# First feed-forward of an attention and two-layer expert chain: operand halves and Strassen sums of the weights kept in DRAM, products chained in PSUM, scores negated

## Chip, cores and metric

The kernel runs on one core of a Trainium2 chip. The metric is the device time of one execution in microseconds (us), as the median of several runs. A change of 0.3% (8.6 us) is about the least that a measurement of this kernel tells from none.

## What is computed

```python
# attention over blocks of 32 queries with 8 memory keys: q, k, v of 4 x 8 heads x 768 x 64
scores = scale * np.matmul(q_c, k_full.transpose(0, 1, 3, 2))
scores = scores - np.max(scores, axis=-1, keepdims=True)
a = np.exp(scores)
a = a / (np.sum(a, axis=-1, keepdims=True) + 1e-09)
out[:, :, c_start:c_end] = np.matmul(a, v_full)
...
# first feed-forward, x is 3072 x 512, w_gate and w_val 512 x 1536, w_out 1536 x 512
gate = 1.0 / (1.0 + np.exp(-(x @ w_gate)))
val = x @ w_val
return (gate * val @ w_out).astype(np.float32)
...
# second: 8 experts of 512 x 1024 x 512, gates P normalised 8 times by rows and columns
h = np.maximum(x @ w1[e], 0.0)
ye = h @ w2[e]
out += P[:, e:e + 1] * ye
```

The weights of the first feed-forward come as float64 (its mean values are made as float64 in the inputs), and the kernel turns them into float32 with integer operations on the chip.

## The kernel before

Every float32 matrix product is made of three matmuls on rounded halves (`mm3`, L74): an operand x is kept as a rounded part h and a rest l = x - h, and `wh*xh + wh*xl + wl*xh` is summed in PSUM. `operand` (L106) makes the two halves: ACT casts h, and another engine (POOL for weights, mostly) subtracts it. "Split" means this below.

The 3072 tokens are 8 chunks of 384 (c = 0 to 7). Attention of a chunk is 4 head pairs (`attention`, L178): score matmuls, DVE scales and masks (L205), takes the row maxima (L208) and negates them (L209), ACT takes the exponential with that bias (L212), DVE the reciprocal of the sums, POOL scales (L216), then transposes and the product with v. It is a generator of four or five pieces, which `hook()` calls at times that `schedule` lists, so that it fills in beside the feed-forward.

**Stage A** (about 0 to 320 us in the trace) has attention of chunks 0 to 3 and the first feed-forward of chunks 0 and 1. `convert(f)` (L250) turns one of 12 groups f of 128 hidden units from float64 to float32: for each of three weights (i = 0 gate, 1 value, 2 out) ACT takes the magnitude, DVE does five operations (L264 to L271), POOL adds (L273), and SP stores the result in the DRAM scratch `wd`. 24 steps follow one another, chunk 0 with f = 0 to 5, chunk 1 with f = 0 to 5, chunk 0 with f = 6 to 11, chunk 1 with f = 6 to 11. `plain_first` (L336) splits the three weights of its step from the float32 tiles in SBUF (for i = 2 and f of 6 or more it loads them from `wd`), does 24 matmuls (`ps`), a sigmoid in three ACT operations (`sg`), and makes `g`, `gh`, `gl`; `plain_second` (L366) does 12 matmuls with the out weight (`px`) one step later. The conversions 2 to 11 stand behind given steps, by the tables

```python
AN = (0, -1, -1, -1, 0, 2, 0, 0, 0, 0)
CV = (0, 1, 2, 3, 6, 8, 9, 11, 12, 14)
```

The k-th conversion is written behind step `CV[k]`, and where `AN[k]` is not negative its DVE work may be issued only after the `gl` of step `CV[k] - AN[k]`.

**Stage B** (about 320 to 862 us) has the first feed-forward of chunks 2 to 7, in three blocks b = 1, 2, 3 of two chunks, and attention of chunks 4 to 7 beside the first two blocks. Each block takes six pairs p of groups f. For a pair, three loads `wl` from `wd` bring the float32 weights; `w1_operands` (L125) makes seven Strassen operands each for gate and value (on POOL four sums of quarters, `combine`, and four splits), and two splits make the out weights. `strassen` (L452) multiplies seven products, each into a PSUM bank of its own (`p_g`, `p_v`), and DVE adds them up (L462, `ca` to `ce`). `second` (L494) does the 48 matmuls with the out weight.

**Behind it** (862 us to the end) come the normalisation of P and the experts. There the second feed-forward already keeps its split operands and Strassen sums in DRAM scratch (`w1k`, `w2k`), reloads them, and chains products in PSUM, with ACT copies (`ca`, `cb`, `ce`, L709 to L720).

Transfers of weights and of q, k, v are all issued by SP, in the order in which the program is laid out. The tile framework orders each engine's instructions, and a buffer's next use waits for its last reader.

Of the kernel before, what the change touches and what calls it, by code (L numbers as in the profile page):

```python
# [10 lines left out]
F32 = mybir.dt.float32  # L11
F32R = mybir.dt.float32r
# [9 lines left out]
QB = 96  # L22
# [38 lines left out]
def moe_chain(ctx: ExitStack, tc: tile.TileContext, qkv, mask, wa, wg, wb, out):  # L61
# [28 lines left out]
    def slot(tag, name, n=512, dt=F32):  # L90
        return big.tile([128, 512], dt, tag=tag, name=name, bufs=SLOTS[tag])[:, 0:n]
# [11 lines left out]
    def tmp(name, n=512):  # L103
        return tp.tile([128, 512], F32, tag="c", name=name)[:, 0:n]
# [39 lines left out]
    def w1_load(nm, pool, kept):  # L144
# [3 lines left out]
        return w1_sets(t)  # L148

    with ExitStack() as c1:  # L150
        wc = c1.enter_context(tc.tile_pool(name="wc", bufs=7))
        wp = c1.enter_context(tc.tile_pool(name="wp", bufs=5))
        un = c1.enter_context(tc.tile_pool(name="un", bufs=2))
# [24 lines left out]
        def attention(c, hp, lead=False):  # L178
# [15 lines left out]
            for j in range(2):  # L194
                p0 = 64 * j
                sc = blocks(psum(f"sc{c}_{hp}_{j}")[:QB])
                for b in range(NBLK):
                    nc.tensor.matmul(sc[:, b, :], qT[p0:p0 + 64, b * QB:(b + 1) * QB],
                                     kv[p0:p0 + 64, b, :], start=True, stop=True)
                if lead:  # L200
                    sm = slot("v", f"sm{c}_{hp}_{j}")
                else:
                    sm = at.tile([128, 512], F32, tag="sm", name=f"sm{c}_{hp}_{j}", bufs=4)
                sm = blocks(sm[:QB])
                nc.vector.scalar_tensor_tensor(out=sm, in0=sc, scalar=0.125, in1=msk[:, c % 2],  # L205
                                               op0=ALU.mult, op1=ALU.add)
                nm = at.tile([QB, NBLK], F32, tag="nm", name=f"nm{c}_{hp}_{j}")
                nc.vector.tensor_reduce(out=nm, in_=sm, axis=AX.X, op=ALU.max)  # L208
                nc.vector.tensor_scalar(out=nm, in0=nm, scalar1=-1.0, scalar2=None, op0=ALU.mult)  # L209
                rs = at.tile([QB, NBLK], F32, tag="rs", name=f"rs{c}_{hp}_{j}")  # L210
                for b in range(NBLK):
                    nc.scalar.activation(sm[:, b, :], sm[:, b, :], AF.Exp, bias=nm[:, b:b + 1],  # L212
                                         scale=1.0, accum_out=rs[:, b:b + 1])
# [31 lines left out]
            yield  # L245

        half = NF1 // 2
        wf = {}

        def convert(f, after=None):  # L250
            for i in range(3):
# [7 lines left out]
                y = tmp(f"y{f}_{i}")  # L259
                r = tmp(f"w{f}_{i}") if i == 2 and f >= half else slot("v" if i == 2 else "w", f"w{f}_{i}")  # L260
                yi, ri = y.bitcast(U32), r.bitcast(U32)
# [50 lines left out]

        def full(pool, nm, src, eng):
            h = pool.tile([128, 512], F32R, tag="ws", name=f"h{nm}")
            l = pool.tile([128, 512], F32R, tag="ws", name=f"l{nm}")
            operand(h, l, eng, src)
            return h, l

        def sigmoid(dst, src, split):
# [16 lines left out]
        def plain_first(c, f):  # L336
            if f >= half:
                if (f, 2, c) not in wf:
                    t = pair(f"wo{c}_{f}")
                    nc.sync.dma_start(out=t[:, 0], in_=wd[f // 2][2][:, f % 2, :])  # L340
                    wf[f, 2, c] = t[:, 0]
                src2 = wf[f, 2, c]
            else:
                src2 = wf[f, 2]
# [107 lines left out]
        def strassen(nm, w, x, temp, emit):  # L452
            p = {}

            def product(i):
                p[i] = bank(f"p{i}_{nm}")[:, 0:CT]
                for kk in range(2):
                    ks = slice(kk * 128, (kk + 1) * 128)
                    mm3(p[i], w[i][0][:, ks], w[i][1][:, ks], *x[i][kk], kk == 0, kk == 1)

            def add(dst, i, src):
                nc.vector.tensor_tensor(out=dst, in0=p[i], in1=src, op=ALU.add)  # L462

            ta, tb = temp("a"), temp("b")
            product(0)
            nc.scalar.copy(ta, p[0])
            yield
            product(5)
            add(tb, 5, ta)
            yield  # L470
            product(1)
            add(ta, 1, ta)
            emit(0, 0, ta)
            yield
            product(6)
            te = temp("e")
            add(te, 6, tb)
            yield
            product(4)
            td = temp("d")  # L480
            add(td, 4, te)
            emit(1, 1, td)
            add(tb, 4, tb)
            yield
            product(2)
            add(tb, 2, tb)
            emit(0, 1, tb)
            yield
            product(3)
            add(te, 3, te)  # L490
            emit(1, 0, te)
            yield
# [20 lines left out]
        for b in range(1, NCH // 2):  # L513
# [3 lines left out]
            for p in range(NPAIR):  # L517
                ld = [pair(f"wl{b}_{p}_{i}") for i in range(3)]
                for i in range(3):
                    nc.sync.dma_start(out=ld[i], in_=wd[p][i])  # L520
                nm = f"{b}_{p}"
                wg_ = w1_operands("g" + nm, ld[0], ws)
                wv_ = w1_operands("v" + nm, ld[1], wc)
                wo = [full(wp, f"wo{nm}_{i}", ld[2][:, i], nc.gpsimd) for i in range(2)]
                sig, gs = {}, {}
# [335 lines left out]
def _mask():  # L861
    m = np.full((QB, 2, NBLK, 128), -3.0e38, np.float32)
    for half in range(2):
# [59 lines left out]
```

## Time and profile before

| | |
|---|---|
| median of 3 runs | 2866.39 us (2864.92 to 2871.77) |
| profiled execution | 2868.21 us, its span 2864.5 us |
| mean granted TensorE clock | 0.976 of full speed |
| busy share of the span | PE 95%, PEld 84%, DVE 74%, ACT 43%, POOL 45% |
| chain that ended last | PE 68%, DVE 14%, DMA 8%, ACT 4%, issue 3%, POOL 3% |

PE is TensorE, PEld its weight loads, DVE VectorE, ACT ScalarE, POOL GpSimd, SP SyncE. The span in 40 slices (71.6 us each) shows where PE is less than full, as the share in tenths: the first four or five slices are stage A, up to slice 12 stage B.

```profile
PE   6778999899998999999999999999998999999999
DVE  8898778888888555455456788888889667677776
POOL 5776677767765233333333333344435222232222
```

In a row of a table by stretch there stand: start:end, its length, busy us and (x instructions) of PE, PEld, DVE, ACT and POOL, the granted clock, the DMA engines' busy share, and GB/s. A row of a tile has the line, engine and operation, the tiles (out<-in) with the count, and the shortest/median/longest duration in ns, then the first and last start in us. A row of the chain or of the timeline begins with start and length in us.

### The profile page before, as it was taken

The numbers are of one execution on the slowest core, as the hardware profiler recorded it, in microseconds if no ns is written. First come the engines' busy times: TensorE is split into PE (matmuls) and PEld (weight loads), VectorE is DVE, ScalarE is ACT, GpSimd is POOL, SyncE is SP. The second block draws the span as 40 slices with busy tenths as digits, with TensorE's granted clock in tenths as the row PEclk, the third lists the DMA queues.
The fourth block names the chain that finished last, engine by engine and source line by source line (L and its number), as shares of the span: only waits on it lengthen the run. The fifth ranks groups of instructions, "written<-read, shape, count | busy, mean of one in ns | idle before, by whom it ended". The sixth has DMA issues, their size and how long they took to land.

```text
span 2864.5 us, 43410 instructions
## 1 busy us (share of the span) xinstructions
PE 2721.6 (95%) x15535; PEld 2410.7 (84%) x15535; DVE 2133.3 (74%) x3349; ACT 1236.0 (43%) x2646; POOL 1292.6 (45%) x1004
## 2 busy tenths in 40 slices
PE   6778999899998999999999999999998999999999
PEld 5677899798995788878787889999997889999998
DVE  8898778888888555455456788888889667677776
ACT  5555666666544333333333333344334333333332
POOL 5776677767765233333333333344435222232222
PEclk8899999999998999999999999999999999999999
DMA  5444222222227355556556656666666645555554
GB/s 175 160 139 134 89 83 92 84 92 74 75 64 264 132 200 209 177 173 211 175 182 201 230 193 234 243 237 220 215 217 212 238 160 208 217 207 201 180 189 184
DMA packets 216568, 499.24 MB, mean 174 GB/s; under 512 B 22464, under 2 KB 39360, under 8 KB 216352
## 3 DMA queue, kind: packets, MB, share of 16 engines
q1 hardware_dynamic: 216352, 496.48, 49.9%
q8 instruction: 122, 2.00, 0.3%
q14 instruction: 94, 0.77, 0.1%
HBM read 348.54 MB, written 147.85 MB: 173 GB/s over the span
## 4 chain that ended last, share of the span: by engine, by line
PE 68%; DVE 14%; DMA 8%; ACT 4%; issue 3%; POOL 3%; SPq 0%; DVEq 0%; POOLq 0%; ACTq 0%
PE p L698 9%; PE p L699 9%; PE p L700 9%; DMA r<-in_wb 4%; PE pzq L799 4%; PE pzq L800 4%; PE pzq L801 4%; PE py L75 3%; PE py L76 3%; PE py L77 3%; PE pzr L799 3%; PE pzr L800 3%; PE pzr L801 3%; DVE gl L108 1%; PE px L76 1%
## 5 line engine op out<-in xcount | busy, mean ns | idle before, releaser
L698 PE MATMUL p<-xh,w 128*128 128x512 f32 x1344 | 529.8, 397 | 20.3 <-ACT ce L720 11.4
L699 PE MATMUL p<-xl,w 128*128 128x512 f32 x1344 | 529.6, 394 | 0.3 <-DVE xl L108 0.3
L700 PE MATMUL p<-xh,w 128*128 128x512 f32 x1344 | 524.9, 393 | 0.8 <-POOL w L108 0.8
L108 POOL TENSOR_TENSOR gl<-ce,gh 128x512 fp32r<-128x512 f32 x64 | 87.7, 1371 | 546.3 <-ACT gh L107 542.0
L698 PEld LDWEIGHTS p<-xh,w 128*128 128x128 f32 x1344 | 255.6, 190 | 73.5 <-ACT ce L720 18.5
L700 PEld LDWEIGHTS p<-xh,w 128*128 128x128 f32 x1344 | 254.8, 190 | 52.2 <-POOL w L108 1.8
L699 PEld LDWEIGHTS p<-xl,w 128*128 128x128 f32 x1344 | 255.4, 190 | 45.1 <-DVE xl L108 0.6
L769 DVE SCALAR_TENSOR_TENSOR acc<-pzr,logit,acc 128x512 f32<-128x512 f32 (+1 forms) x362 | 200.9, 572 | 90.8 <-PE pzr L801 89.9
L769 DVE SCALAR_TENSOR_TENSOR acc<-pzq,logit,acc 128x512 f32<-128x512 f32 x244 | 176.7, 745 | 54.9 <-PE pzq L801 51.8
L76 PE MATMUL py<-w2b,gh 128*128 128x512 f32 x528 | 206.0, 390 | 0.0
L75 PE MATMUL py<-w2a,gh 128*128 128x512 f32 x528 | 205.5, 391 | 0.0
L108 POOL TENSOR_TENSOR sl<-cb,sh 128x512 fp32r<-128x512 f32 (+1 forms) x64 | 87.5, 1368 | 255.3 <-ACT sh L107 245.5
L77 PE MATMUL py<-w2a,gl 128*128 128x512 f32 x528 | 201.4, 390 | 0.0
L108 POOL TENSOR_TENSOR w2b<-r,w2a 128x1024 fp32r<-128x1024 f32 x32 | 77.7, 2429 | 260.1 <-ACT w2a L107 260.1
L675 ACT ACTIVATE gh<-ca 128x512 fp32r<-128x512 f32 x96 | 60.6, 631 | 274.6 <-PE pzr L800 131.6
L703 DVE TENSOR_TENSOR cd<-p,ce 128x512 f32<-128x512 f32 x96 | 65.8, 686 | 127.5 <-ACT ce L720 126.9
L799 PE MATMUL pzr<-w2c,sh 128*128 128x256 f32 x504 | 142.3, 283 | 2.9 <-DVE acc L769 2.5
L800 PE MATMUL pzr<-w2d,sh 128*128 128x256 f32 x504 | 142.2, 283 | 0.0
L801 PE MATMUL pzr<-w2c,sl 128*128 128x256 f32 x504 | 140.8, 283 | 0.0
L769 DVE SCALAR_TENSOR_TENSOR acc<-py,logit,acc 128x512 f32<-128x512 f32 x116 | 84.9, 747 | 71.9 <-PE py L77 71.7
L212 ACT ACTIVATE sm<-sm,nm 96x128 f32<-96x128 f32 x256 | 99.7, 391 | 60.6 <-DVE nm L209 55.3
L108 POOL TENSOR_TENSOR w<-wq,w 128x512 fp32r<-128x512 f32 x64 | 85.9, 1345 | 85.0 <-ACT w L107 70.6
(283 smaller groups left out, 8373.2 us busy)
## 6 DMA issues: line engine op xcount, KB each, us to landing
w<-w1k SPq DMA_DIRECT2D x448, 256.0 KB, 5.3
w1k<-w SPq DMA_DIRECT2D x224, 256.0 KB, 3.8
r<-in_wb SPq DMA_DIRECT2D x96, 512.0 KB, 5.4
w2a<-w2k SPq DMA_DIRECT2D x64, 512.0 KB, 5.1
w2b<-w2k SPq DMA_DIRECT2D x64, 512.0 KB, 6.1
wl<-wd SPq DMA_DIRECT2D x54, 512.0 KB, 3.3
u<-in_qkv SPq DMA_DIRECT2D x28, 704.0 KB, 4.6
raw<-in_wa SPq DMA_DIRECT2D x36, 512.0 KB, 4.2
```

What stands on the lines that cost most here:

```text
L75: nc.tensor.matmul(ps, wh, xh, start=first, stop=False)
L76: nc.tensor.matmul(ps, wh, xl, start=False, stop=False)
L77: nc.tensor.matmul(ps, wl, xh, start=False, stop=last)
L108: return eng.tensor_tensor(out=l, in0=src, in1=h.bitcast(F32), op=ALU.subtract)
L212: nc.scalar.activation(sm[:, b, :], sm[:, b, :], AF.Exp, bias=nm[:, b:b + 1], scale=1.0, accum_out=rs[:, b:b + 1])
L698: nc.tensor.matmul(ps, wh[:, ks], xh, start=kk == 0 and not more, stop=False, skip_group_check=True)
L699: nc.tensor.matmul(ps, wh[:, ks], xl, start=False, stop=False, skip_group_check=True)
L700: nc.tensor.matmul(ps, wl[:, ks], xh, start=False, stop=kk == 1, skip_group_check=True)
L769: nc.vector.scalar_tensor_tensor(out=dst, in0=src, scalar=pe, in1=dst, op0=ALU.mult, op1=ALU.add)
L799: nc.tensor.matmul(ps, gh[:, cs], wh, start=fp == 0 and not more, stop=False, skip_group_check=True)
L800: nc.tensor.matmul(ps, gh[:, cs], wl, start=False, stop=False, skip_group_check=True)
L801: nc.tensor.matmul(ps, gl[:, cs], wh, start=False, stop=fp == 1, skip_group_check=True)
```

## The change

There are four parts.

1. `convert` splits each weight as soon as it is float32 (ACT casts, POOL subtracts) and stores both halves in a DRAM scratch `whl` (256 KB each, 72 in all). Of the float32 weights only gate and value are still stored in `wd` (24 stores, not 36). Chunk 0 with f below 6 uses the halves in SBUF; the other 18 steps load six halves each from `whl` (108 loads). The 12 loads of out weights from `wd` go, and so do the splits in `plain_first`.
2. In stage B the plain operands of a pair are loaded from `whl`. For b = 1 `w1_first` still makes the sums (six POOL operations for each of gate and value, not eight) and stores their halves in `wcd`; for b = 2 and 3 `w1_again` loads all seven tiles. The out weights are four loads per pair. The pool `wp` has 6 buffers, not 5.
3. `strassen` goes through the products in the order 0, 1, 5, 4, 6, 3, 2. 0, 5 and 6 are summed in one PSUM bank (`chain`), 4 and 2 in another (`right`). Per call there are four DVE adds in place of seven, and three ACT copies in place of one.
4. The scores are kept negated: the scale is -0.125, the mask +3e38, the reduction a minimum, so that it is the bias of the exponential, and L209 goes (64 times).

```diff
-    wd = [[dr.tile([128, 2, 512], F32, name=f"wd{p}_{i}") for i in range(3)] for p in range(NF1 // 2)]
+    wd = [[dr.tile([128, 2, 512], F32, name=f"wd{p}_{i}") for i in range(2)] for p in range(NF1 // 2)]
+    whl = [[dr.tile([128, 2, 512], F32, name=f"whl{f}_{i}") for i in range(3)] for f in range(NF1)]
...
+    def load_plain(t, plain):
+        nc.sync.dma_start(out=flat(t[0]).bitcast(F32), in_=plain[0][:, 0, :])
+        nc.sync.dma_start(out=flat(t[1]).bitcast(F32), in_=plain[0][:, 1, :])
+        nc.sync.dma_start(out=t[6].bitcast(F32), in_=plain[1][:, :, 256:512])
+
+    def w1_again(nm, pool, plain, kept):
+        t = w1_tiles(nm, pool)
+        load_plain(t, plain)
+        for k in range(4):
+            nc.sync.dma_start(out=flat(t[2 + k]).bitcast(F32), in_=kept[k])
+        return w1_sets(t)
...
-                nc.vector.tensor_reduce(out=nm, in_=sm, axis=AX.X, op=ALU.max)
-                nc.vector.tensor_scalar(out=nm, in0=nm, scalar1=-1.0, scalar2=None, op0=ALU.mult)
+                nc.vector.tensor_reduce(out=nm, in_=sm, axis=AX.X, op=ALU.min)
...
+        def split_load(pool, nm, kept):
+            h = pool.tile([128, 512], F32R, tag="ws", name=f"h{nm}")
+            l = pool.tile([128, 512], F32R, tag="ws", name=f"l{nm}")
+            nc.sync.dma_start(out=h.bitcast(F32), in_=kept[:, 0, :])
+            nc.sync.dma_start(out=l.bitcast(F32), in_=kept[:, 1, :])
+            return h, l
...
-                nc.sync.dma_start(out=wd[f // 2][i][:, f % 2, :], in_=r)
-                wf[f, i] = r
+                if i < 2:
+                    nc.sync.dma_start(out=wd[f // 2][i][:, f % 2, :], in_=r)
+                h, l = full((ws, wc, wp)[i], f"w{i}_0_{f}", r, nc.gpsimd)
+                nc.sync.dma_start(out=whl[f][i][:, 0, :], in_=h.bitcast(F32))
+                nc.sync.dma_start(out=whl[f][i][:, 1, :], in_=l.bitcast(F32))
+                if f < GS:
+                    wf[f, i] = h, l
...
-            wt = [full((ws, wc, wp)[i], f"w{i}_{c}_{f}", src2 if i == 2 else wf[f, i],
-                       nc.vector if i == 1 and f >= half else nc.gpsimd) for i in range(3)]
+            wt = [wf.pop((f, i)) if c == 0 and (f, i) in wf else split_load((ws, wc, wp)[i], f"w{i}_{c}_{f}_r", whl[f][i])
+                  for i in range(3)]
...
             product(0, chain)
             nc.scalar.copy(ta, chain)
...
             product(5, chain, True)
             nc.scalar.copy(tb, chain)
             yield
             right = bank(f"p4_{nm}")[:, 0:CT]
             product(4, right)
             yield
             product(6, chain, True)
             te, td = temp("e"), temp("d")
             nc.scalar.copy(te, chain)
             add(td, right, te)
...
             product(2, right, True)
             add(tb, right, tb)
```

Where the instructions stand is seen in the order of each engine. On POOL, where chunk 1 takes up the feed-forward, there stood before (`lw0_1_3` is the rest half of weight 0 for chunk 1, f = 3; `sm` is a scaling of attention):

```order
L216 TENSOR_TENSOR sm1_3_1_1266<-sm1_3_1_1266,rs1_3_1_1271 96x512
L108 TENSOR_TENSOR lw0_1_0_1594<-w0_0_668,hw0_1_0_1593 128x512
L108 TENSOR_TENSOR lw1_0_5_1538<-w5_1_1452,hw1_0_5_1537 128x512
L108 TENSOR_TENSOR lw0_1_1_1714<-w1_0_704,hw0_1_1_1713 128x512
L108 TENSOR_TENSOR lw1_1_0_1598<-w0_1_680,hw1_1_0_1597 128x512
L108 TENSOR_TENSOR lw0_1_2_1796<-w2_0_964,hw0_1_2_1795 128x512
L108 TENSOR_TENSOR lw1_1_1_1718<-w1_1_716,hw1_1_1_1717 128x512
...
```

and now

```order
L315 TENSOR_TENSOR w5_1_1557<-y5_1_1556,w5_1_1557 128x512
L110 TENSOR_TENSOR lw0_0_5_1549<-w5_0_1539,hw0_0_5_1548 128x512
L110 TENSOR_TENSOR lw1_0_5_1567<-w5_1_1557,hw1_0_5_1566 128x512
L315 TENSOR_TENSOR w5_2_1575<-y5_2_1574,w5_2_1575 128x512
L245 TENSOR_TENSOR sm2_0_0_1752<-sm2_0_0_1752,rs2_0_0_1756 96x512
L110 TENSOR_TENSOR lw2_0_5_1584<-w5_2_1575,hw2_0_5_1583 128x512
L245 TENSOR_TENSOR sm2_0_1_1851<-sm2_0_1_1851,rs2_0_1_1855 96x512
L315 TENSOR_TENSOR w6_0_1771<-y6_0_1770,w6_0_1771 128x512
```

The run of 13 splits, most of them for chunk 1, is gone; the splits stand singly behind the addition of their conversion, and attention's scalings between them.

On SP, about the last conversion (f = 11), there stood before only loads of raw weights, of q, k, v (`u`) and of single out weights (`wo`) beside the stores:

```order
L340 DMA wo0_9_2661<-wd4_2_92 128x512
L340 DMA wo0_10_2786<-wd5_2_95 128x512
L188 DMA u3_1_2688<-in_qkv 128x1408
L274 DMA wd5_0_93<-w11_0_2628 128x512
L274 DMA wd5_1_94<-w11_1_2640 128x512
L274 DMA wd5_2_95<-w11_2_2652 128x512
L340 DMA wo0_11_2868<-wd5_2_95 128x512
```

and now (`hw0_0_9_r` and `lw0_0_9_r` are the halves of the gate weight of chunk 0, f = 9, which is step 15)

```order
L286 DMA lw2_0_8_r_2724<-whl8_2_116 128x512
L560 DMA wl1_0_3737<-wd0_1_79 128x1024
L317 DMA wd5_0_88<-w11_0_2789 128x512
L319 DMA whl11_0_123<-hw0_0_11_2798 128x512
L285 DMA hw0_0_9_r_2839<-whl9_0_117 128x512
L317 DMA wd5_1_89<-w11_1_2807 128x512
L319 DMA whl11_1_124<-hw1_0_11_2816 128x512
L286 DMA lw0_0_9_r_2840<-whl9_0_117 128x512
L285 DMA hw1_0_9_r_2843<-whl9_1_118 128x512
```

The weights of step 15, whose halves lie in DRAM since conversion 9, are now issued behind two stores of conversion 11, whose DVE work is issued behind the `gl` of step 14 (`gl0_8`). Of the other steps of this kind (7, 10, 12, 13 and 17) the same holds with an earlier conversion.

On PE, between the two matmul groups of steps 6 and 7 (`ps1_1_0` is the value of chunk 1, f = 0, `ps0_1_1` the gate of f = 1), there stood before

```order
L77 MATMUL ps1_1_0_1618<-xh1_3_1411,lw1_1_0_1598 128x384
L198 MATMUL sc2_0_1_1738<-u2_0_1653 96x128 x4
L76 MATMUL px0_0_0_1092<-gl0_5_1578,hw2_0_5_1541 128x384
...
L77 MATMUL px0_0_3_1095<-gh0_5_1577,lw2_0_5_1542 128x384
L198 MATMUL sc2_1_0_1835<-u2_1_1833 96x128 x4
L75 MATMUL ps0_1_1_1725<-xh1_0_1058,hw0_1_1_1713 128x384
```

and now

```order
L77 MATMUL ps1_1_0_1710<-xh1_3_1510,lw1_1_0_r_1690 128x384
L228 MATMUL sc2_1_0_1942<-u2_1_1940 96x128 x4
L253 MATMUL pt2_0_0_1981<-ident_58,sm2_0_0_1752 128x96 x4
L253 MATMUL pt2_0_1_1988<-ident_58,sm2_0_1_1851 128x96 x4
L228 MATMUL sc2_1_1_1995<-u2_1_1940 96x128 x4
L266 MATMUL po2_0_2090<-pT2_0_0_1986,u2_0_1745 64x96 x4
L266 MATMUL po2_0_2090<-pT2_0_1_1993,u2_0_1745 64x96 x4
L228 MATMUL sc2_2_0_2216<-u2_2_2214 96x128 x4
L253 MATMUL pt2_1_0_2246<-ident_58,sm2_1_0_1947 128x96 x4
L75 MATMUL ps0_1_1_1833<-xh1_0_1151,hw0_1_1_r_1821 128x384
```

More than a head pair of attention has moved in between the two groups; the matmuls of step 7 start behind it.

## Rows read from the trace of the kernel before

**Rows 1.** Work by stretch: stage A in three parts, then stage B

```profile
0.00:143.00 143.00, 102.51 (x586) 88.69 (x587) 118.96 (x201) 78.27 (x235) 89.98 (x69) 0.82 0.52 168
143.00:250.00 107.00, 84.59 (x503) 77.71 (x502) 99.69 (x165) 59.03 (x166) 73.14 (x42) 0.95 0.45 148
250.00:320.00 70.00, 66.58 (x415) 61.34 (x414) 48.58 (x76) 45.46 (x126) 40.98 (x35) 0.95 0.31 102
320.00:862.00 542.00, 515.58 (x3089) 482.07 (x3087) 458.61 (x775) 319.59 (x849) 392.58 (x372) 0.98 0.24 81
```

**Rows 2.** Waits of PE in stage A: us in total, times, longest

```profile
PE ps L75 <- DVE g L357: 8.7, 7, 2.2
PE px L76 <- DVE gl L108: 7.5, 6, 2.6
```

**Rows 3.** Timeline of POOL and DVE, 120 to 142 us

```profile
124.66 14.90 POOL L108 TENSOR_TENSOR lw<-w,hw 128x512 fp32r<-128x512 f32 x12
...
134.39 5.59 DVE L108 TENSOR_TENSOR gl<-g,gh 128x384 fp32r<-128x384 f32 x1
```

**Rows 4.** Tiles gl and nm up to 862 us, on DVE

```profile
L108 DVE TENSOR_TENSOR gl<-g,gh x24: 524/550/6356, 59.7 to 321.9; 128x384 fp32r<-128x384 f32 x24
...
L209 DVE TENSOR_SCALAR nm<-nm x64: 128/166/4182, 9.0 to 692.7; 96x4 f32<-96x4 f32 x64
```

**Rows 5.** DVE groups up to 862 us: busy us, mean ns | idle before

```profile
L209 DVE TENSOR_SCALAR nm<-nm 96x4 f32<-96x4 f32 x64 | 37.4, 584 | 0.4
```

**Rows 6.** Chain that ended last, 200 to 262 us

```profile
225.59 5.15 DVE w L271
230.81 1.26 POOL w L273
232.16 4.22 DMA wd<-w
...
244.56 3.72 DMA wo<-wd
248.30 0.62 ACT hw L107
```

**Rows 7.** Tiles y and w of the conversion in stage A

```profile
L264 DVE TENSOR_SCALAR y<-y x36: 386/412/2293, 18.0 to 239.1; 128x512 f32<-128x512 f32 x36
...
L268 DVE SCALAR_TENSOR_TENSOR y<-raw,y x36: 654/677/4778, 21.0 to 241.7; 128x512 uint32<-128x512 uint32 x36
...
L273 POOL TENSOR_TENSOR w<-y,w x36: 1259/1292/3119, 29.9 to 254.1; 128x512 f32<-128x512 f32 x36
...
L271 DVE SCALAR_TENSOR_TENSOR w<-raw,w x36: 650/678/5136, 25.8 to 246.4; 128x512 f32<-128x512 uint32 x36
```

**Rows 8.** Loads of single weight tiles, 143 to 250 us: count, KB, us to landing

```profile
wo<-wd SPq DMA_DIRECT2D x5, 256.0 KB, 3.6
```

**Rows 9.** Chain that ended last, 0 to 320 us: attention on PE

```profile
189.42 1.19 PE po L237 x16
...
277.62 1.04 PE sc L198 x8
```

**Rows 10.** Work by stretch: a busy stretch of DMA, and a dense one of PE

```profile
10.00:20.00 10.00, 4.92 (x50) 4.40 (x47) 9.69 (x27) 9.05 (x41) 4.26 (x4) 0.95 1.04 409
750.00:800.00 50.00, 50.00 (x286) 49.70 (x287) 39.39 (x64) 20.79 (x42) 38.02 (x37) 1.00 0.19 64
```

**Rows 11.** Work by stretch: the three Strassen blocks of stage B

```profile
320.60:522.10 201.50, 187.74 (x1144) 172.76 (x1143) 175.84 (x290) 127.22 (x360) 150.03 (x142) 0.97 0.25 85
522.10:712.70 190.60, 182.12 (x1121) 168.47 (x1120) 160.42 (x281) 119.77 (x335) 140.15 (x133) 0.98 0.25 82
712.70:862.20 149.50, 145.32 (x824) 140.24 (x822) 121.95 (x206) 72.20 (x156) 102.20 (x100) 1.00 0.23 73
```

**Rows 12.** Tile p_g: the DVE adds and ACT copies on a product

```profile
L462 DVE TENSOR_TENSOR cgb<-p_g,cgb x36: 522/548/560, 336.1 to 838.4; 128x384 f32<-128x384 f32 x36
L466 ACT COPY cga<-p_g x18: 467/471/479, 322.9 to 832.5; 128x384 f32<-128x384 f32 x18
```

**Rows 13.** Waits of PE in the second feed-forward, 950 to 2865 us

```profile
PE p L698 <- ACT ce L720: 11.2, 15, 2.1
```

More of the change, by code (lines that the diff above doesn't have):

```diff
@@ L148, in w1_load, with w1_first @@
         return w1_sets(t)
+    def w1_first(nm, r, pool, plain, kept):
+        a11, a12, a21, a22 = (r[:, i, kh * 256:(kh + 1) * 256] for i in range(2) for kh in range(2))
+        t = w1_tiles(nm, pool)
+        ge = nc.gpsimd
+        q = quad(f"wq{nm}")
+        load_plain(t, plain)
+        combine(ge, q[:, 0], a21, a22, ALU.add)
+        combine(ge, q[:, 1], q[:, 0], a11, ALU.subtract)
+        operand(t[2], t[3], ge, q[:, 0:2])
+        combine(ge, q[:, 2], a11, a21, ALU.subtract)
+        combine(ge, q[:, 3], a12, q[:, 1], ALU.subtract)
+        operand(t[4], t[5], ge, q[:, 2:4])
+        for k in range(4):
+            nc.sync.dma_start(out=kept[k], in_=flat(t[2 + k]).bitcast(F32))
+        return w1_sets(t)
[4 more added lines that the diff above has]
+    def w1_again(nm, pool, plain, kept):
+        t = w1_tiles(nm, pool)
+        load_plain(t, plain)
+        for k in range(4):
+            nc.sync.dma_start(out=flat(t[2 + k]).bitcast(F32), in_=kept[k])
+        return w1_sets(t)
     with ExitStack() as c1:
         wc = c1.enter_context(tc.tile_pool(name="wc", bufs=7))
[L152 removed]
+        wp = c1.enter_context(tc.tile_pool(name="wp", bufs=6))
         un = c1.enter_context(tc.tile_pool(name="un", bufs=2))
@@ L259, in convert @@
                 y = tmp(f"y{f}_{i}")
-                r = tmp(f"w{f}_{i}") if i == 2 and f >= half else slot("v" if i == 2 else "w", f"w{f}_{i}")
+                r = slot("w", f"w{f}_{i}")
                 yi, ri = y.bitcast(U32), r.bitcast(U32)
@@ L452, in strassen, with product @@
         def strassen(nm, w, x, temp, emit):
-            p = {}
-            def product(i):
-                p[i] = bank(f"p{i}_{nm}")[:, 0:CT]
+            def product(i, ps, more=False):
                 for kk in range(2):
                     ks = slice(kk * 128, (kk + 1) * 128)
-                    mm3(p[i], w[i][0][:, ks], w[i][1][:, ks], *x[i][kk], kk == 0, kk == 1)
-            def add(dst, i, src):
-                nc.vector.tensor_tensor(out=dst, in0=p[i], in1=src, op=ALU.add)
+                    (wh, wl), (xh, xl) = w[i], x[i][kk]
+                    nc.tensor.matmul(ps, wh[:, ks], xh, start=kk == 0 and not more, stop=False, skip_group_check=True)
+                    nc.tensor.matmul(ps, wh[:, ks], xl, start=False, stop=False, skip_group_check=True)
+                    nc.tensor.matmul(ps, wl[:, ks], xh, start=False, stop=kk == 1, skip_group_check=True)
@@ L464, in strassen, with add @@
+            def add(dst, ps, src):
+                nc.vector.tensor_tensor(out=dst, in0=ps, in1=src, op=ALU.add)
             ta, tb = temp("a"), temp("b")
-            product(0)
-            nc.scalar.copy(ta, p[0])
+            chain = bank(f"p0_{nm}")[:, 0:CT]
+            product(0, chain)
+            nc.scalar.copy(ta, chain)
             yield
[L468 to L472, printed above, removed]
+            other = bank(f"p1_{nm}")[:, 0:CT]
@@ L473, in strassen @@
+            product(1, other)
+            add(ta, other, ta)
             emit(0, 0, ta)
             yield
-            product(6)
-            te = temp("e")
-            add(te, 6, tb)
+            product(5, chain, True)
+            nc.scalar.copy(tb, chain)
             yield
-            product(4)
-            td = temp("d")
-            add(td, 4, te)
+            right = bank(f"p4_{nm}")[:, 0:CT]
+            product(4, right)
+            yield
+            product(6, chain, True)
+            te, td = temp("e"), temp("d")
@@ L482, in strassen @@
+            nc.scalar.copy(te, chain)
+            add(td, right, te)
             emit(1, 1, td)
-            add(tb, 4, tb)
             yield
-            product(2)
-            add(tb, 2, tb)
+            other = bank(f"p3_{nm}")[:, 0:CT]
+            product(3, other)
+            add(te, other, te)
+            emit(1, 0, te)
+            yield
+            product(2, right, True)
+            add(tb, right, tb)
             emit(0, 1, tb)
-            yield
-            product(3)
-            add(te, 3, te)
@@ L517, in moe_chain @@
             for p in range(NPAIR):
-                ld = [pair(f"wl{b}_{p}_{i}") for i in range(3)]
-                for i in range(3):
-                    nc.sync.dma_start(out=ld[i], in_=wd[p][i])
                 nm = f"{b}_{p}"
-                wg_ = w1_operands("g" + nm, ld[0], ws)
-                wv_ = w1_operands("v" + nm, ld[1], wc)
-                wo = [full(wp, f"wo{nm}_{i}", ld[2][:, i], nc.gpsimd) for i in range(2)]
+                wgv = []
+                for i in range(2):
+                    plain = whl[2 * p][i], whl[2 * p + 1][i]
+                    n, pool = "gv"[i] + nm, (ws, wc)[i]
+                    if b == 1:
+                        ld = pair(f"wl{i}_{p}")
+                        nc.sync.dma_start(out=ld, in_=wd[p][i])
+                        wgv.append(w1_first(n, ld, pool, plain, wcd[p][i]))
+                    else:
+                        wgv.append(w1_again(n, pool, plain, wcd[p][i]))
+                wg_, wv_ = wgv
+                wo = [split_load(wp, f"wo{nm}_{i}", whl[2 * p + i][2]) for i in range(2)]
                 sig, gs = {}, {}
@@ L861, in _mask @@
 def _mask():
-    m = np.full((QB, 2, NBLK, 128), -3.0e38, np.float32)
+    m = np.full((QB, 2, NBLK, 128), 3.0e38, np.float32)
     for half in range(2):
```

24 lines of the change are left out of this document (8 added, 16 removed).

## The prediction

> **What bounds the kernel now.** I read the work by stretch first. Over the whole span PE is at 95%, so what can be won is where PE is less than full. In stage A it idles 143 - 102.5 = 40.5, 22.4 and 3.4 us in the three parts, in stage B 26.4 us [rows 1]; DVE is there at 83%, 93%, 69% and 85%. Next, the waits of PE in stage A: the operations that it waits for are `g` and `gl` on DVE [rows 2], so PE is held by a busy DVE, not by transfers. The chain that ended last says the same: between 225 and 250 us it runs through DVE's conversion, POOL, a store, and a reload [rows 6].
>
> DVE is longer busy than its work is. `gl` has a median of 550 ns and a maximum of 6356 [rows 4]. The timeline shows one such case: at 124.7 POOL begins twelve splits that end at 139.6, and `gl`, begun at 134.4, ends when they do, 5.59 us later [rows 3]. The small negation of the maxima has a median of 166 ns but a mean of 584 [rows 4, 5]. DVE operations that read only SBUF stand still while POOL runs through a row of operations; those that read a PSUM product do not (522 to 560 ns over 36) [rows 12]. So POOL work is paid on DVE, in stage B too, where POOL is busy 392.6 of 542 us [rows 1].
>
> The Trainium skill ("SBUF — State Buffer", section "Who interferes with whom") has this as a lock that one instruction of either engine holds for its whole length. The trace agrees on who waits, but 5.59 us is more than four POOL operations of 1.24 us, not one: by the rule alone a wait would end after 1.3 us, the longest would be 1.9 us, and the first term below would come to about -6 in place of -10.
>
> **The sum**, against the profiled 2868.2 us (1.8 above the median of the runs).
>
> *Term 1, 0 to 143 us.* The row of splits for chunk 1 disappears from POOL. That gives back the stall of `gl`, 5.59 - 0.55 = 5.0 us, with PE waiting behind it. The negation goes: about 18 of its 64 are here, 18 × 0.584 = 10.5 us of DVE, of which I count half on the path, 5. Each conversion still has three POOL splits, as the first six groups had. Term: **-10**. Bounds: nothing if another DVE operation takes the stall over, and -25 if all of the negation and 10 us of the conversions' own stalls (one of L271 took 5.15 [rows 6], its median is 0.678 [rows 7]) go too.
>
> *Term 2, 143 to 320 us.* Here the change adds a chain. The halves that a step needs were made from SBUF; now they are loads that stand in SP's order behind the stores of a conversion, and this behind the `gl` of the step before. At steps 7, 10, 12, 13, 15 and 17: DVE's fifteen operations up to the first L271 take 3 × 0.412 + 3 × 0.412 + 3 × 0.677 + 3 × 0.412 + 0.678 = 6.4 us (the other two short operations taken as L264), POOL's addition 1.29 [rows 7], the cast 0.62 [rows 6]; then the store is issued and the load behind it lands 3.6 us later [rows 8]. Together 11.9 us from `gl` to the weights. PE meanwhile has the 12 `px` matmuls of the step before, 12 × 0.175 = 2.1 us (0.175 is 50 us over 286 [rows 10]), and one head pair of attention, which the order has moved into such a gap: 2 × 1.04 + 1.19 [rows 9] and eight transposes at the 0.074 of a `po` matmul, 3.9 us. What is left is 5.9 us per place. Before, the ten steps of 143 to 250 us cost 22.4 us of idle PE, 2.2 each [rows 1]. So 6 × (5.9 - 2.2) = 22 more. Against this: 24 fewer POOL splits and 12 fewer DVE splits in stage A, and the rest of the negation; I take 7 off. Term: **+15**. Bounds: with two head pairs in every gap the stall is 2.0, no more than before, and the relief counts 10: -10. With no attention to fill in: 9.8 - 2.2 = 7.6, six times, +45.
>
> In this stretch the transfers grow too: 148 GB/s over 107 us is 15.8 MB [rows 1]; six conversions store 6 × 6 × 0.262 = 9.4 MB more, 63 of the 108 loads bring 16.5, four `u` of 0.72 come earlier, 2.9, and some 2.9 of `wd` and `wo` go: 41.7 MB. At the 409 GB/s that the queues reach at 10 to 20 us [rows 10] this is 102 us of 107, so it just fits; I count nothing, and up to 21 us in a rival.
>
> The Trainium skill ("DMA: Bandwidth & Descriptors", section "Specifications") gives about 358 GB/s as a core's share of HBM, by which the stretch would want 116 us, 9 more than it has. The trace shows 409 GB/s for 10 us, above that figure.
>
> *Term 3, stage B.* The matmuls are 36 × 42 + 18 × 48 = 2376 at 0.175 = 416 us. Attention is 16 × 3.9 = 62, logits and the tail of stage A 58 matmuls, 10. That leaves 542 - 488 = 54 us of loss: 26.4 in which PE idles, the rest in matmuls that start late. By blocks, each with 792 matmuls = 138.6 us: the third loses 149.5 - 138.6 = 11 [rows 11], the first two the other 43. POOL now makes 36 × 8 + 36 = 324 of its 372 operations for weights, afterwards 12 × 6 = 72. At 392.6 / 372 = 1.055 us [rows 1] this takes 266 us off POOL and leaves 127. DVE loses 108 adds of 0.544 us (59) and 32 negations of 0.584 (19): 458.6 to 381 before any stall shortens. With both engines relieved, the loss should fall, but the operands of the three blocks' beginnings (`xl` on POOL and DVE) and the starts of a block remain. The third block, without attention, still loses 11, and two or three such starts are some 30 us of the 54. I take the middle of 10 and 54: **-32**. Bounds -10 (only the third of PE's idle time that has to do with weights) and -54 + 10 = -44.
>
> The loads are 18 per pair of 0.26 MB, 4.7 MB in some 30 us, 157 GB/s, against 409 that the queues reached [rows 10]; hidden, since a pair's tiles come free in steps through the pair before. If they came late by one landing of 3.6 us at each of 18 pairs, it would be 65 us, and the term would turn round; nothing in the rows asks for that.
>
> *Term 4, chained products.* 72 ACT copies come in, 0.471 each [rows 12], 34 us on an ACT that is busy 319.6 of 542 us and loses 36 + 120 casts of weights. A product that goes on in the same bank must wait for the copy; in the order at least six other matmuls (1.05 us) stand between, more than 0.47. In the second feed-forward, with the same form, PE waits 11.2 us in 15 cases for a copy [rows 13], over some 192 copies of that kind, two in each of 96 calls; the 72 here in proportion are **+4**. Bounds 0, and +16 if ACT with its sigmoids is four times as late.
>
> Sum: -10 + 15 - 32 + 4 = -23, profiled 2845, median **2843 us**.
>
> **The rivals.**
>
> *R1, the queue (other side).* One mechanism: SP issues a step's loads only behind a conversion's stores. If attention has run out or itself waits for `u` behind these stores, the stall per place is 9.8, plus the arrival of the four halves that `ps` needs, 1.05 MB at 409 GB/s = 2.6: 12.4 - 2.2 = 10.2, six times 61, less 7. Then -10 + 54 - 32 + 4 = +16: 2882 us. For it: in the order nothing else of PE is left but attention. Against: two head pairs were moved into the gap shown. It decides from 38 us in term 2, a stall of 9.7 per place.
>
> *R2, transfers.* 41.7 MB at 80% of 409 GB/s take 128 us, 21 more than the stretch: with a part hidden by term 2's waits, +14: 2857 us. For it: bursts of loads and stores stand together. Against: queues reached 409.
>
> *R3, all of the stalls go.* Term 1 -20, term 2 at 0, term 3 -45, term 4 +4: -61, 2805 us. For it: DVE's excess lies everywhere where POOL has a row. Against: the third block's loss without attention or conversions.
>
> *R4, nothing.* PE is the bound and DVE's relief in stage B goes to time that PE did not wait for: PE's idle 26.4 us there stays with the `x` operands of block starts, and term 2 takes back term 1: 2866 us.
>
> **How the numbers follow.** Forecast 0.38 (own range 2828 to 2857), R1 0.20, R2 0.12, R3 0.20, R4 0.10. The bound of what can be told from no change is 0.3%, 8.6 us. R2 lies at the edge and counts half as faster: faster 0.38 + 0.20 + 0.06 = 0.64, same 0.16, slower 0.20. The range reaches to R3 and R1, leaving the outer part of each: 2806 to 2880.
>
> **What would show it.** Term 1: `gl` without a case of 5 us, the 143 us stretch shorter by 10. Term 2: PE waiting for `hw` or `lw` from DMA at steps 7 to 17, 4 to 6 us each, and the time between the sigmoids of steps 7 and 17 longer. Term 3: stage B at 505 to 515 us, POOL near 127 us in it, mean of the gated products' splits (`gl<-cva`, `gl<-cvb`) near 550 ns. Term 4: waits of `p_g` or `p_v` for copies below 10 us in all. The prediction is wrong if stage B keeps its length though POOL falls, which would mean that PE's loss there has another cause, or if stage A grows by more than 38 us.

## The result, and the profile after

The changed kernel takes 2891.0 us (median of 4 runs, 2889.8 to 2893.1) where the one before takes 2865.8 beside it: ratio 1.0084, 95% interval 1.0067 to 1.0102. It is 25 us slower. The forecast was 2843 with a range up to 2880.

The profiled execution's span is 2888.0 us. By stretches, columns as in [rows 1] (the last row is stage B, from its first product to the last `px`):

```profile
0.00:143.00 143.00, 103.39 (x588) 90.85 (x588) 113.85 (x193) 77.41 (x239) 73.35 (x60) 0.82 0.69 234
143.00:250.00 107.00, 72.36 (x406) 64.59 (x407) 70.88 (x119) 47.54 (x147) 43.93 (x34) 0.74 0.69 241
250.00:320.00 70.00, 43.83 (x215) 39.95 (x214) 24.09 (x52) 21.10 (x55) 26.63 (x25) 0.70 0.67 236
...
370.60:890.40 519.80, 507.13 (x3085) 478.46 (x3085) 337.61 (x648) 283.08 (x775) 126.74 (x121) 0.99 0.60 198
```

Against [rows 1], PE does 406 and 215 instructions in the second and third stretch, where it did 503 and 415, and the granted clock there is 0.74 and 0.70, not 0.95. Stage B starts at 370.6 us, 50 us later, lasts 519.8 instead of 541.2, and what follows takes 1997.6 instead of 2002.7: +50.0 - 21.4 - 5.1 = +23.5, the difference of the spans. POOL in stage B is at 127 us, DVE at 338.

Five intervals of stage A, from one step's sigmoid to the next, take most of the time (pauses, below). They are those of steps 7, 10, 12, 13 and 15, whose sigmoids end each row:

```profile
138.70:176.50 37.80, 21.04 (x112) 17.98 (x110) 33.47 (x50) 14.95 (x50) 19.06 (x14) 0.68 0.65 222
187.30:219.90 32.60, 23.21 (x139) 20.29 (x137) 17.01 (x35) 14.50 (x48) 13.07 (x10) 0.74 0.65 224
224.10:254.10 30.00, 20.34 (x114) 17.78 (x113) 20.20 (x35) 14.80 (x50) 12.19 (x10) 0.73 0.52 173
254.10:284.30 30.20, 15.48 (x81) 13.23 (x81) 12.82 (x26) 9.64 (x29) 10.05 (x9) 0.61 0.68 250
291.50:313.80 22.30, 10.84 (x50) 10.02 (x49) 7.75 (x17) 3.94 (x8) 13.40 (x14) 0.69 0.51 166
```

Together 152.9 us; before, the same five intervals took 6.2, 8.0, 9.6, 7.8 and 16.7, together 48.3. From the sigmoid of step 6 to that of step 23 it is 228.4 us (174.7 before), so all other steps together became 50.9 faster: the conversions and attention that lay beside them now stand in these five pauses (of attention's product with v, `po`, 107 matmuls fall into the five, 15 before).

The pause of step 13 shows how. On DVE and POOL, from `gl` on:

```profile
259.32 0.56 DVE L110 TENSOR_TENSOR gl<-g,gh 128x384 fp32r<-128x384 f32 x1 [0.58 <-ACT gh L109]
259.80 1.09 DVE L306 TENSOR_SCALAR y<-y 128x512 f32<-128x512 f32 x3
...
270.13 1.23 DVE L313 SCALAR_TENSOR_TENSOR w<-raw,w 128x512 f32<-128x512 uint32 x1
```

```profile
267.93 2.88 POOL L315 TENSOR_TENSOR w<-y,w 128x512 f32<-128x512 f32 x2 [13.60 <-DVE w L313]
```

On SP, then on PE:

```profile
256.17 11.79 SPq L218 DMA_DIRECT2D u<-in_qkv  x2
268.05 0.86 SPq L298 DMA_DIRECT2D raw<-in_wa  x2
269.62 0.33 SPq L317 DMA_DIRECT2D wd<-w  x1
271.39 0.33 SPq L560 DMA_DIRECT2D wl<-wd  x1
271.81 0.43 SPq L319 DMA_DIRECT2D whl<-hw  x1
272.33 0.60 SPq L317 DMA_DIRECT2D wd<-w  x1
272.98 0.55 SPq L285 DMA_DIRECT2D hw_r<-whl  x1
```

```profile
265.35 2.24 PE L266 MATMUL po<-pT,u 128*64 128x96 f32 x16
279.55 0.69 PE L75 MATMUL ps<-xh,hw_r 128*128 128x384 f32 x1 [11.96 <-DMA hw_r<-whl]
280.03 0.52 PE L76 MATMUL ps<-xl,hw_r 128*128 128x384 f32 x1
280.35 0.55 PE L77 MATMUL ps<-xh,lw_r 128*128 128x384 f32 x1
```

The conversion's fifteen DVE operations begin when `gl` is done and last until 271.4, since six operations of attention stand among them; SP issues `u` and raw loads that wait for buffers (the last of these waits ends at 268.5), two stores of that conversion, the second behind the third of POOL's additions (272.7), and only then, at 273.0, the first half for step 13, which has lain in DRAM for a long time and lands 6.5 us later. Since the matmuls of step 12 PE has done some one and a half head pairs of attention, and it stands for 12.0 us. Then its matmuls start 0.32 us apart, not 0.175, up to 285.5: from 279.55 to 285.5 the granted clock is 0.50, the lower of the two levels (1.2 of 2.4 GHz), 2.5 us more in this pause.

From the end of `gl` to the landing of the next step's first half, the five pauses take 20.7, 21.2, 17.9, 19.6 and 12.3 us. PE waits for that half itself in three of them, steps 7, 13 and 15 (5.0, 12.0 and 9.9 us):

```profile
PE ps L75 <- DMA hw_r<-whl: 26.8, 3, 12.0
```

At steps 10 and 12 the half lands 2.2 and 1.5 us before PE comes to it, since the attention ahead of it on PE has waited too (6.2 us for a `u` load, 4.7 us for POOL's scaling). Attention fills the pauses only in part: PE's waits for it from 138.7 to 313.8 us add up to 31 us.

The splits of the gated products show what the change did give. The maximum of `gl<-g` was 6356 ns [rows 4], and in stage B there stood before

```profile
L108 DVE TENSOR_TENSOR gl<-cva,gh x18: 540/981/1959, 350.1 to 845.7; 128x384 fp32r<-128x384 f32 x18
```

Now they are

```profile
L110 DVE TENSOR_TENSOR gl<-g,gh x24: 543/559/1353, 60.6 to 371.3; 128x384 fp32r<-128x384 f32 x24
...
L110 DVE TENSOR_TENSOR gl<-cva,gh x18: 544/558/2520, 387.0 to 868.9; 128x384 fp32r<-128x384 f32 x18
```

### The profile page after: what moved, and what is told of

It is laid out like the page before. It is cut to its first block, busy times and chain, and to the rows that moved or that the text cites. A ratio compares the mean times of both kernels' runs of the same rounds, so it can differ in the third digit from the quotient of the medians.

```text
span 2888.0 us, 43666 instructions
## 1 busy us (share of the span) xinstructions
PE 2722.7 (94%) x15535; PEld 2421.9 (84%) x15535; DVE 1963.9 (68%) x3165; ACT 1182.3 (41%) x2526; POOL 970.1 (34%) x728
## 4 chain that ended last, share of the span: by engine, by line
PE 79%; DVE 9%; DMA 7%; issue 2%; ACT 2%; POOL 1%; SPq 1%; DVEq 0%; POOLq 0%; ACTq 0%
PE p L739 9%; PE p L740 9%; PE p L741 9%; PE pzq L840 4%; PE pzq L842 4%; PE pzq L841 4%; PE py L75 3%; PE py L76 3%; PE py L77 3%; DMA r<-in_wb 3%; PE pzr L841 3%; PE pzr L842 3%; PE pzr L840 3%; PE px L76 2%; PE px L75 2%
## 5 line engine op out<-in xcount | busy, mean ns | idle before, releaser
L739 PE MATMUL p<-xh,w 128*128 128x512 f32 x1344 | 528.4, 396 | 21.7 <-ACT ce L761 11.6
L110 POOL TENSOR_TENSOR w2b<-r,w2a 128x1024 fp32r<-128x1024 f32 x32 | 77.6, 2425 | 268.6 <-ACT w2a L109 268.5
L245 POOL TENSOR_TENSOR sm<-sm,rs 96x512 f32<-96x512 f32 x64 | 73.5, 1150 | 235.5 <-DVE rs L244 154.1
## 6 DMA issues: line engine op xcount, KB each, us to landing
r<-in_wb SPq DMA_DIRECT2D x96, 512.0 KB, 5.5
w2a<-w2k SPq DMA_DIRECT2D x64, 512.0 KB, 4.7
w2b<-w2k SPq DMA_DIRECT2D x64, 512.0 KB, 5.8
raw<-in_wa SPq DMA_DIRECT2D x36, 512.0 KB, 5.7
w2k<-w2a SPq DMA_DIRECT2D x32, 512.0 KB, 2.6
```

The source lines that it names most:

```text
L110: return eng.tensor_tensor(out=l, in0=src, in1=h.bitcast(F32), op=ALU.subtract)
L739: nc.tensor.matmul(ps, wh[:, ks], xh, start=kk == 0 and not more, stop=False, skip_group_check=True)
```

## The experiments

Stage A below ends with the first `p_g` matmul, stage B with the last `px`; its blocks are b1 to b3. These are the profiled executions, in us; `median` is that of the runs.

| kernel | median | A | b1 | b2 | b3 | B | behind |
|---|---|---|---|---|---|---|---|
| before | 2865.8 | 320.6 | 201.5 | 190.6 | 149.1 | 541.2 | 2002.7 |
| changed | 2891.0 | 370.6 | 186.2 | 182.9 | 150.7 | 519.8 | 1997.6 |
| e1, split in SBUF | 2839.3 | 318.9 | 186.2 | 184.2 | 150.7 | 521.1 | 1995.7 |
| e2, loads by POOL | 2905.8 | 387.5 | 189.0 | 181.3 | 150.6 | 520.9 | 1994.9 |
| e2, stores by POOL | 2910.2 | 388.1 | 194.2 | 181.6 | 150.7 | 526.5 | 1993.8 |
| e4, q-k-v loads by ACT | 2901.7 | 380.5 | 191.0 | 182.9 | 150.3 | 524.2 | 1991.6 |
| e3, no anchors | 2857.6 | 320.8 | 207.4 | 181.7 | 151.7 | 540.8 | 1996.4 |
| e10, loads a step earlier | 2859.7 | 339.2 | 187.2 | 182.9 | 150.7 | 520.8 | 2001.0 |
| e13, both of these | 2851.3 | 316.8 | 207.1 | 181.3 | 151.3 | 539.7 | 1992.9 |
| e5, before + negation | 2846.8 | 315.3 | 195.1 | 185.8 | 146.9 | 527.8 | 2001.3 |
| e6, before + chain | 2881.0 | 316.6 | 205.2 | 196.9 | 157.4 | 559.5 | 1999.7 |
| e7, changed - chain | 2876.8 | 370.2 | 183.9 | 177.7 | 142.9 | 504.5 | 2000.3 |
| e9, e1 - chain | 2826.6 | 318.0 | 184.2 | 177.5 | 143.1 | 504.8 | 1999.9 |
| e12, e1, last pairs unchained | 2837.7 | 326.1 | 186.5 | 180.8 | 143.6 | 510.9 | 2001.5 |

**Is it the reload at all (e1)?** `convert` and the splits of `plain_first` are those of before; chunk 0's steps store the halves for stage B:

```diff
+            if c == 0:
+                for i in range(3):
+                    for k in range(2):
+                        nc.sync.dma_start(out=whl[f][i][:, k, :], in_=wt[i][k].bitcast(F32))
```

> Stage A as before the change (the weights of both chunks are split from the float32 tiles in SBUF, no reload of halves), and chunk 0's steps store their halves for stage B, which is that of the changed kernel. Queue theory (the 50 us of stage A are lost because the loads of a step's halves stand in SP's order behind a conversion's stores): the first product of stage B starts at 320 to 328 us as before, stage B lasts 520, the whole 2845 to 2855. Traffic theory (the added transfers slow everything): the 72 stores remain, so a good part of the loss remains, first product at 335 to 350, the whole 2860 to 2875.

2839.3 us, ratio to before 0.9902 (0.9885 to 0.9918), below what either theory expected. Stage A is back at 318.9 us, stage B keeps its gain. The traffic theory falls with it, since stage A here moves 218 and 190 GB/s where before it was 148 and 102 [rows 1]:

```profile
143.00:250.00 107.00, 92.22 (x524) 85.03 (x523) 102.67 (x155) 58.67 (x158) 67.17 (x42) 0.88 0.65 218
250.00:320.00 70.00, 63.54 (x400) 58.00 (x398) 46.89 (x67) 45.44 (x125) 45.80 (x42) 0.96 0.57 190
```

**Which place in the queues? (e2, e2, e4.)** Three moves of DMAs to another engine:

```diff
-        def split_load(pool, nm, kept):
+        def split_load(pool, nm, kept, q=None):
...
-            nc.sync.dma_start(out=h.bitcast(F32), in_=kept[:, 0, :])
...
+            (q or nc.sync).dma_start(out=h.bitcast(F32), in_=kept[:, 0, :])
...
+            wt = [wf.pop((f, i)) if c == 0 and (f, i) in wf else split_load((ws, wc, wp)[i], f"w{i}_{c}_{f}_r", whl[f][i], nc.gpsimd)
```

> The changed kernel with the 108 loads of halves in stage A issued by POOL in place of SP. Queue theory: the loads no longer stand behind stores and u loads, the intervals before steps 7, 10, 12, 13 and 15 fall from 22 to 38 us to 10 to 15, first product of stage B at 320 to 345 in place of 371, the whole 2840 to 2865. Traffic theory: the same bytes in the same time, first product at 360 to 375, the whole 2880 to 2895. If POOL's own order makes the loads wait (for a scaling of attention or a conversion's addition) something between.

```diff
-                nc.sync.dma_start(out=whl[f][i][:, 0, :], in_=h.bitcast(F32))
+                nc.gpsimd.dma_start(out=whl[f][i][:, 0, :], in_=h.bitcast(F32))
...
```

> The changed kernel with the conversions' stores issued by POOL, behind the split that it has just done; SP keeps the raw loads, q-k-v loads and the loads of halves. If the stores in SP's queue hold the loads up (the form of the rival that I priced), first product of stage B at 325 to 345, the whole 2845 to 2868. If it is the raw loads and the q-k-v loads ahead of them in SP, or the anchors behind gl, that hold them, little changes: first product at 360 to 375, the whole 2880 to 2895.

```diff
-                nc.sync.dma_start(out=u, in_=qkv[c, hp])
+                nc.scalar.dma_start(out=u, in_=qkv[c, hp])
```

> The changed kernel with the q-k-v loads issued by ACT in place of SP. SP waited 66 us in nine of these for their buffers, which the product with v sets free. If that is what holds the conversions' raw loads and so the halves' loads up: first product of stage B at 330 to 350, the whole 2850 to 2870. If the stores or the anchors do it: 360 to 375 and 2880 to 2895. ACT itself may be held by the same buffers: then slower than 2895.

All three are slower than the changed kernel, by 11 to 19 us, with pauses of 19 to 38 us before the same five steps. The three narrow forms of the queue theory (these stores, these `u` loads, SP alone) all fall. In the first, the loads stand on POOL behind the conversion's additions (POOL waits 63.8 us, between 100 and 390, for the DVE work before them, and each of the 108 issues takes POOL some 0.55 us, a cost that no run takes apart from the order); in the second, SP holds them behind the raw loads, which wait for the buffers of the conversion before:

```profile
151.32 22.13 SPq L218 DMA_DIRECT2D u<-in_qkv  x2
176.15 5.79 SPq L298 DMA_DIRECT2D raw<-in_wa  x4
182.04 0.37 SPq L285 DMA_DIRECT2D hw_r<-whl  x1
```

What is common in the orders is that a conversion's raw load, addition or store stands ahead of the next step's halves in whichever queue carries them. That leaves the order itself.

**Opening the loop (e3, e10, e13).** e3 takes the hold of the conversions behind `gl` away, e10 writes the loads of a step's halves ahead of the conversion in between, e13 does both:

```diff
-AN = (0, -1, -1, -1, 0, 2, 0, 0, 0, 0)
+AN = (-1, -1, -1, -1, -1, -1, -1, -1, -1, -1)
```

> The changed kernel with no conversion held back until a step's gl (all of AN at -1); loads stay in SP's queue. Queue theory: the loop of step, conversion, store and load is opened at one point, conversions run ahead, first product of stage B at 335 to 355, the whole 2855 to 2875; if the loads still stand behind stores whose raw weights come late, less. Traffic theory: no change, 2885 to 2895. If the conversions now hold up gl and the maxima on DVE it could also be slower.

```diff
...
             prev = c, f, st
+            if i + 1 < len(steps):
+                prefetch(*steps[i + 1])
             for k, n in conv.get(i, ()):
                 convert(k, anchor[i - n] if n >= 0 else None)
```

> The changed kernel with the loads of a step's six halves written one step earlier, ahead of the conversion that stands between the two steps; all still in SP's queue, with the same stores, raw loads and anchors. Order theory (a step's loads are laid behind everything of the conversion in between, its raw loads, its work and its stores, whichever queue they are in, and the conversion behind the step before): the pauses before steps 7, 10, 12, 13 and 15 shrink from 22 to 38 us to under 15, first product of stage B at 320 to 345, the whole 2840 to 2865. If it is the tile buffers that the conversion's halves and the loaded halves share, or DVE's work of the conversions itself, that sets the pace: first product at 360 to 375, the whole 2880 to 2895.

> The changed kernel with the loads of halves written a step earlier and without the anchors of the conversions. If both open the same loop (each gave 31 to 33 us), the two together give little more than one: 2845 to 2860. If the order of the loads and the hold of the conversions are two separate losses: 2825 to 2842. If conversions that run ahead of gl on DVE hurt where loads are early: above 2865.

2857.6, 2859.7 and 2851.3 us: each alone takes 31 to 33 us off the changed kernel, both together 40. So it is a loop: step, conversion behind its `gl`, loads behind the conversion, next step. Opening it at either point gives most of the loss back; to e1, 12 us are still missing with both, and what they are was not settled. In e3 stage A ends 50 us earlier, but block 1 is then 21 us longer, so that 29 us are left at the end of stage B. Part of this is work that moved: up to the first `p_g` PE does 1428 instructions in e3 and in e13, not the 1504 of the changed kernel (the transposes and products with v of two head pairs, the scores of one and the logits are missing), and they stand in block 1. Stage A of these two is thus shorter partly by having less to do; e10 has 1503. In e10 four of the five intervals fall to 3 to 8 us, but that of step 13 stays at 28.8: its first half is issued at 225.0, still behind stores of the conversion further back, and PE waits 8.0 us for it. That e3 moves 317 GB/s from 143 to 250 us, more than the changed kernel's 241, and is faster, speaks again against traffic:

```profile
143.00:250.00 107.00, 83.89 (x453) 75.72 (x454) 78.23 (x121) 51.09 (x141) 60.02 (x49) 0.83 0.91 317
```

**The negation alone (e5)** is the kernel before with part 4.

> The kernel before with the negated scores alone. My first term counted some 5 us for it in the first 143 us, and 19 us of DVE work in stage B: by that 2855 to 2862. If the negation only took the waits that the next DVE operation now takes, no change, 2862 to 2870.

2846.8, ratio 0.9928 (0.9911 to 0.9944), some 20 us faster and below both expectations: 13.4 in stage B, and 5.3 in stage A, which is less than one stage A differs from another (below). The 20 us are more than the 64 × 0.166 = 10.6 us that the operations take undisturbed; of the 37.4 us that they held DVE [rows 5], the rest was waiting.

**The chain (e6, e7, e9, e12).** e6 puts the new `strassen` into the kernel before, e7 and e9 put the old one into the changed kernel and into e1.

> The changed kernel with the old strassen (each product in its own bank, seven DVE adds and one ACT copy per call). My forecast priced the copies at +4 and counted the 59 us of adds in stage B's gain: if DVE's work is what stage B lost by, stage B goes from 520 to 530 or more and the whole to 2900. If POOL's work was it, stage B stays within 3 us, the whole at 2885 to 2895. If the chained form costs PE waits, the whole falls below 2885.

> The kernel before with the chained products alone. From the difference of 13 to 14 us that the chain made in two pairs of kernels (2891 against 2877, 2839 against 2827) it costs 13 here too: 2875 to 2885. If on the busy DVE of the kernel before the 59 us of adds that it saves are worth something, less: 2860 to 2872.

> Both findings together: stage A splits from SBUF (first experiment, 2839) and the old strassen (14 us less in the changed kernel). If the two are independent, 2839 - 14 = 2825; if the chain's cost hung on stage A's late end, 2836 to 2842.

In all three pairs the chained form loses: 2881.0 against 2868.1 (ratio 1.0054, 1.0037 to 1.0072), 2891.0 against 2876.8, 2839.3 against 2826.6; in stage B 15 to 18 us. PE's waits in stage B of the changed kernel are for the last gated products of a block:

```profile
PE px L76 <- DVE gl L110: 6.6, 4, 3.0
PE px L75 <- ACT gh L109: 4.3, 3, 3.2
```

In the order on PE at the end of block 3, all 72 last `px` matmuls stand behind the value's seven products without the chain (e7); in the changed kernel 36 stand between the products, so only 36 are left to cover the wait for the last `gh` and `gl`. e12 tries this: the old form in the last pair of each block alone.

```diff
+        def strassen(nm, *a):
+            return (strassen_own if nm.endswith(f"_{NPAIR - 1}") else strassen_chain)(nm, *a)
```

> The first experiment's kernel (2839) with the old strassen in the last pair of each block only, the chained form in the other fifteen pairs. If the chain costs its 13 us at the block ends, where the matmuls that covered the last products are laid between the chained ones and gh and gl are waited for: 2826 to 2830, as with the old form everywhere (2827). If each pair pays for its ACT copies, a sixth of it: 2836 to 2839.

The total, 2837.7, told against the block ends; in the trace stage B had become 10 us shorter and stage A, in the same order, 7 us longer. Hence the three kernels once more on one chip:

> The first experiment's kernel again, on one chip with the next two: 2837 to 2842.

> The kernel with the old strassen in the last pair of each block alone, on the same chip as the chained and the unchained one. By its trace stage B had become 10 us shorter, but its whole was no less, with a stage A of the same order 7 us longer. If that was the chip or the execution, it comes out between the two others here, 4 to 10 us below the chained one; if the end of the blocks has no part in the cost, within 2 us of the chained one.

> Stage A split from SBUF, old strassen everywhere, again: 2824 to 2829, 11 to 14 below the chained one.

2841.9, 2838.1 and 2831.4 us; stage B 519.8, 512.0 and 505.7, while stage A was 327.4, 318.8 and 323.9. Stage A of one order varies by some 9 us from execution to execution, stage B by 1. So of the chain's 15 us in stage B the ends of the blocks make 8 to 10 (7 in b3, nothing in b1); behind stage B, 3 to 4 us come back in three of the four pairs, little more than the 2.4 by which that stretch differs between e1 and its repeat. Of the other 5 to 7 us, in the first two blocks, the trace says only where they lie: from e15 to e16 PE is busy 3.5 us less there for the same matmuls and idle 2.4 us less. What delays them was not settled.

**The best version** is e9: halves and sums kept for stage B, negated scores, stage A split from SBUF, products unchained. 2826.6 us, ratio 0.986 (0.9842 to 0.9878); again 2831.4, ratio 0.9877 (0.9858 to 0.9896). Its stage B leaves PE 2 us idle:

```profile
318.00:822.80 504.80, 502.65 (x3084) 476.86 (x3083) 376.62 (x746) 251.44 (x698) 125.80 (x119) 1.00 0.61 204
```

## Why the prediction was wrong, step by step

- *Term 1* (-10) came to -4: the sigmoid of step 6 ends at 138.7 us, not 142.4. That is less than the spread of one kernel (133.0 in e1, 140.2 in its repeat), so the size of this term is not shown. The stall of `gl` went. The reading behind it, that PE is held by DVE and not by transfers, rested on two of the waits. The longest in stage A is another, for ACT's cast of `g`:

```profile
PE px L75 <- ACT gh L107: 10.7, 4, 4.3
```

- *Term 2* (+15, bounds -10 to +45) is the step that failed: +54, from the sigmoid of step 6 to that of step 23. The chain and its places were right (five of the six that I named), the size per place was not: I had 3.7 us more at each, and it is 104.6 / 5 = 21, of which the steps between give 51 us in all back. From `gl` to the weights I put 11.9 us; in the pause of step 13 it is 279.5 - 259.9 = 19.6, and 18.3 in the mean of the five. The conversion took DVE 11.6 us, not 6.4: I had counted up to the first of its three last operations (8.0 us here), but the second store ahead of the load waited for the third; and the attention that I let fill PE's gap needs DVE in the midst of the conversion. The load landed after 6.5, not 3.6. SP's `u` and raw loads, which I had left out, stand ahead too, though in this pause they do not end last. I took attention as 3.9 us of work without waits of its own. The low clock (0.61 to 0.74 over the five pauses) was in no term.
- *R1*, the rival that I gave 0.20, had the mechanism. That its +54 for term 2 is the measured number is luck: it had 10.2 us more at each of six places and 7 back, where 21 at each of five and 51 back were measured. Its narrow form was wrong: with the stores out of SP's queue nothing is won. It is the order of conversion and loads together with the anchors.
- *R2*, transfers: refuted as the limit of the stretch by e1 and e3; what is left of it is that a half lands in 5.4 us, not 3.6, in the bursts. The Trainium skill ("DMA: Bandwidth & Descriptors", section "Specifications") has about 358 GB/s for a core's share of HBM; from 320 to 350 us this kernel moved 390 with PE busy 29.3 of 30 us, so here the measured rate stands above that figure:

```profile
320.00:350.00 30.00, 29.32 (x172) 28.69 (x171) 13.60 (x26) 12.70 (x28) 3.86 (x3) 1.00 1.05 390
```

- *Term 3* (-32) holds: without the chain stage B is 504.5 us, -36.7. The negation alone is -13.4 of it (e5), the kept operands by subtraction the other -23.3. That the 59 us of DVE adds were part of the gain is wrong: without them saved, stage B is at its shortest. *R4* (PE's idle time in stage B stays) is refuted: without the chain it is 2 us, before 26.4. *R3* had term 3 rightly larger, but term 2 at 0.
- *Term 4* (+4, bounds 0 to +16) was mis-sized at +15: the waits of single copies are few, but the order pays with the matmuls that covered a block's end.

The sum as measured, by the spans: +50.0 in stage A, -36.7 + 15.3 in stage B, -5.1 behind.

## What to carry to other kernels

A value that is reloaded instead of rebuilt is cheap only if its load is laid ahead of the work that it doesn't depend on: before counting bytes, read in each queue what stands in front of the load, and follow that back to see whether it waits for the very step that the load is for. Work that fills a gap on one engine is no filler if it uses the engine on which the gap's cause runs. Several edits in one change are to be timed one by one: here the negation (-20) and the kept sums (-23 in stage B) were covered by the reload (+50 in stage A) and the chain (+13).

## What was unexpected of the hardware

- A DVE operation of 0.17 us cost more than its length: taking 64 negations away (10.6 us at their median, busy 37.4 us in all, [rows 5]) made the kernel 20 us faster. The Trainium skill ("SBUF — State Buffer", section "Who interferes with whom") says that of DVE and POOL the one that holds their shared port pair blocks the other for its whole operation; no run here takes POOL's part in the 20 us apart from the shorter chain from score to exponential.
- After a standstill of 12.0 us the matmuls start 0.32 us apart, from 280.0 to 285.5 us, at a granted clock of 0.50; from 286 us it is 1.00. Over 250 to 320 us it was 0.70, against 0.95 before.
- The landing of 256 KB loads rose from 3.6 us (median in [rows 8]) to 5.4 (143 to 320 us), with the DMA engines' mean share below 0.7 there. The mean hides the bursts: from 268 to 279.5 us, where the first half of step 13 is under way, the share is 0.91.
- In this trace SP never has more than eight transfers under way. From 275.7 us on in the pause of step 13 the issues wait for that, each going out as the one eight before it lands (275.67 us after a landing at 275.66), so that slower landings delay the issues too.
